# Both products of every join in the third PSUM bank of the MLP, and all steps in a new order

## The chip, the cores and the metric

The kernel runs on one NeuronCore of a Trainium2 chip. The metric is the device time of one execution, in microseconds (us). A kernel is run several times, and its time is the median of the runs. One further execution is profiled by the hardware; its span, clock and single instructions are what the views of the profile show.

The engines are called as in the profile: PE (TensorE matmuls), PEld (its weight loads), DVE (VectorE), ACT (ScalarE), POOL (GpSimd), SP (SyncE, which issues most of the DMAs). A "q" behind the name (SPq, ACTq) is that engine's issuing of DMAs. L856 is line 856 of the kernel.

## The reference, cut to what matters

Four batches, eight heads, 768 tokens, head dimension 48. A DeltaNet recurrence gives x, and an MLP with layer norm and residual works on it:

```python
k_n = k / (norm(k) + 1e-6)
for t in range(768):
    y[t]  = q[t] @ state
    v_old = k_n[t] @ state
    state = state + beta[t] * outer(k_n[t], v[t] - v_old)
x  = y as (4, 768, 384)
xn = (x - mean) / sqrt(var + 1e-6) * g_ln
out = x + maximum(xn @ w_ch1, 0) @ w_ch2      # 384 -> 1536 -> 384
```

All is float32.

## The kernel before

**Chunks.** The tokens are handled in 12 chunks of 64 (all 32 pairs of batch and head at once). Inside a chunk the recurrence is written as a triangular system: the Gram matrix of the keys (`gram`, L786) is stored to HBM and read back in another layout (tile `gb`, eight DMAs on SP, L830), and `rows_inverse` (L822) inverts the two 32x32 diagonal blocks of two chunks at a time, with 31 pairs of VectorE operations one behind the other (the product into `tmp`, L856, and the subtraction from `xb`, L863). The result is stored (`xd`, L867) and read back by DMAs on SP into `xt` (L870). All DMAs go through one helper and so have the line L349.

**The join.** `join(c)` (L879) makes the off-diagonal block of the inverse from the two diagonal ones: a VectorE transpose into `xnj` (L884), 64 matmuls of 32x32 (`prod_e`, L894, called e2 for chunk 2 and so on), four ACT multiplications by -1 into `es` (L906), 64 matmuls again (`prod_z`, L900, called z2), and four ACT copies into `xt` (L912). Both products stand in one PSUM bank, `bank`. Chunks 1 to 5 take `f_[2]`, the third bank of the MLP; from `LATER` = 6 on they take `by[:, 0]`, the first half of the two banks that the recurrence uses for Y.

**The recurrence.** `recur(c)` (L967) has the products keys times state (ks, in `two`) and queries times state (qs, in `by`), both L979, the subtraction from v, the product with the inverse (u, L1013), then the output (y, L1020, in `by`) and the new state (s, L1030, in `two`). The products of queries and keys of a chunk (L771) use `by` too. These, like the join's, are many matmuls on small tiles (64 or 32 wide).

**The MLP.** For chunks 0 to 3 the first layer is a plain product (L1296). From chunk `FROM` = 4 on it is done in fifteen block products on sums of blocks, `fifteen(c)` (L1168): each product is eight matmuls of 128x128 (L1217), and they accumulate in the four banks `f_[2], f_[1], f_[0], f_[3]` (`X`, L1208); products 0, 3, 5 and 8 go to `f_[2]`, and what is in a bank is added up by ACT copies (L1233) and VectorE sums (L1237) into `h_all`. The second layer is done in seven products, `seven(c)` (L1398): each is six steps of two matmuls, 128x192 wide (L1419), in `f_[0]`, `f_[3]`, `f_[1]` for these chunks. Their sums of inputs run on POOL (L1406) or VectorE.

**The order.** Every step is registered with the keys that it reads and writes (`Line.add`, L169); there are 2991. They are issued in the sequence written out in `ORDER` (L59 to 153), in which `z` stands for a filler matmul (`zeros`, L1511). A step can stand anywhere behind those that it depends on, by its keys. `in_this_order` (L26) then pins the queue of each engine to that sequence, with the issues of DMAs in it, so on each engine nothing overtakes. Each MLP step of PE can be put between the steps of the recurrence of the next chunk, and `ORDER` does so nearly everywhere.

**The first inverse.** Chunk 0 has its own inverse, made by doubling on PE (`first_inverse`, L648, products at L720 and L737) in two halves of the heads, g0 and g1. The masks that it needs are made by VectorE (L395, L402) and Pool (L421) in the first ten microseconds. The first `rows_inverse` is that of chunk 1; then come chunks 2 and 3 together, 4 and 5, and so on.

Of the kernel before, what the change touches and what calls it, by code (L numbers as in the profile page):

```python
# [63 lines left out]
146 232 230 149 326 150 219 669 154 z 209 234 155 156 208 231 233 210 158 157 251 46 235 164 160 162 327 200 161 328 239 201 411 159 413 165 170 166  # L64
# [136 lines left out]
def kernel(  # L201
# [26 lines left out]
    FROM, LATER = 4, 6  # L228
# [72 lines left out]
    by = psum.tile([128, 2, 512], FP32, name="by")  # L301
# [20 lines left out]
    ATT = FK[2]  # L322
# [1326 lines left out]
```

## Time and profile before

| what | us |
|---|---|
| median of 3 runs | 508.59 (508.59, 509.01, 507.37) |
| profiled execution | 506.83 |
| its span | 505.1 (1.73 lie around it) |
| PE busy in the span | 485.9 |
| DVE busy | 355.2 |
| POOL busy | 275.7 |
| ACT busy | 249.0 |
| mean granted PE clock | 0.973 |

The chain of work that ended last lies on PE for 78% of the span and on DVE for 13%; 31% of the span is L1419 and 22% is L1217. The DVE part is the inverse (L856 and L863, 4% each), all of it in the first quarter of the span.

A few steps can be followed by their times in the trace. The first tensor operation of the inverse of chunk 1 starts at 35.5 us, its last pass ends at 72.2; that of chunks 2 and 3 starts at 81.3 and ends at 113.7; their reloaded blocks have landed at 123.0, and e2 starts at 123.8. Later joins: e4 at 183.7, e6 at 244.8, e7 at 276.7, e8 at 331.6, e9 at 356.3, e10 at 402.3, e11 at 424.7 us.

In views of groups a row has the line, engine, operation, output and input tiles, the shapes, the count and the durations. In the view of waits a row has the engine and line that waited, what ended the wait, and the total, the number and the longest. In the chain a row has the start, the length and the work.

### The profile page before, as it was taken

What the parts mean: (1) busy time and instruction counts of PE and PEld (TensorE: products, weight loads), DVE (VectorE), ACT (ScalarE), POOL (GpSimd) and SP (SyncE); (2) the same over time, 40 slices, a digit from 0 to 9 for tenths busy, and PEclk for the clock granted to TensorE, in tenths of its full rate; (3) what the DMA queues carried; (4) which work ended last, traced back from release to release, by engine and by line L of the source; (5) the groups of instructions that cost most, each with busy time, mean ns of one, the idle gap of its engine ahead of it and who ended that gap; (6) DMA issues with size and microseconds to landing.
All of it is one profiled execution on the core that took longest, in us unless ns stands there. A gap on an engine that the chain in (4) does not pass through costs nothing.

```text
span 505.1 us, 22184 instructions
## 1 busy us (share of the span) xinstructions
PE 485.9 (96%) x9606; PEld 445.7 (88%) x9606; DVE 355.2 (70%) x774; ACT 249.0 (49%) x620; POOL 275.7 (55%) x430
## 2 busy tenths in 40 slices
PE   6777999999999999999999999999999999999996
PEld 3666988688988898899999999999999999999996
DVE  9689987997699458886559898478899238143251
ACT  5777772633645434636444544436563347363230
POOL 5464527255754595629893462591642851645643
PEclk9776799999999999999999999999999999999999
DMA  8979896756646676448734434765245412111101
GB/s 173 308 153 187 270 189 79 107 138 133 90 87 106 192 127 114 46 100 205 155 41 64 102 55 153 150 91 87 57 85 136 82 23 58 43 50 46 31 12 31
DMA packets 196097, 54.99 MB, mean 109 GB/s; under 512 B 186076, under 2 KB 189404, under 8 KB 196000
## 3 DMA queue, kind: packets, MB, share of 16 engines
q1 hardware_dynamic: 189920, 40.58, 42.1%
q10 hardware_dynamic: 3872, 9.83, 6.1%
q0 software_dynamic: 2208, 3.17, 3.7%
q8 instruction: 75, 1.23, 1.0%
q14 instruction: 22, 0.18, 0.1%
HBM read 36.64 MB, written 16.91 MB: 106 GB/s over the span
## 4 chain that ended last, share of the span: by engine, by line
PE 78%; DVE 13%; SPq 3%; issue 2%; POOL 1%; DMA 1%; ACT 1%; ACTq 0%; DVEq 0%; POOLq 0%
PE f L1419 31%; PE f L1217 22%; PE f L1296 6%; DVE xb L863 4%; DVE tmp L856 4%; SPq L349 3%; PE by L1020 2%; PE two L1013 2%; PE by L979 2%; PE by L771 2%; PE two L979 2%; PE two L1030 1%; PE two L771 1%; PE by L894 1%; PE by L900 1%
## 5 line engine op out<-in xcount | busy, mean ns | idle before, releaser
L1406 POOL TENSOR_TENSOR h_all<-h_all 128x256 f32<-128x256 f32 x123 | 90.2, 746 | 133.3 <-PE f L1419 103.7
L1419 PE MATMUL f<-w_sb,h_all 128*128 128x192 f32 x492 | 109.5, 332 | 0.0
L1419 PE MATMUL f<-words,h_all 128*128 128x192 f32 x396 | 84.5, 330 | 0.3 <-POOL h_all L1406 0.3
L1419 PEld LDWEIGHTS f<-w_sb,h_all 128*128 128x128 f32 x492 | 81.8, 190 | 1.8 <-DVE o L1437 0.2
L863 DVE TENSOR_TENSOR xb<-xb,tmp 128x87 f32<-128x87 f32 (+21 forms) x186 | 73.7, 396 | 4.8
L856 DVE TENSOR_TENSOR tmp<-xb,gb 128x87 f32<-128x87 f32 (+21 forms) x186 | 73.1, 393 | 4.9
L1237 DVE TENSOR_TENSOR h_all<-h_all,f 128x512 f32<-128x512 f32 x96 | 63.6, 682 | 14.2 <-PE f L1217 13.1
L1419 PEld LDWEIGHTS f<-words,h_all 128*128 128x128 f32 x396 | 66.6, 190 | 1.7 <-POOL h_all L1406 1.0
L1296 PE MATMUL f<-xnt,w_sb 128*128 128x256 f32 x216 | 50.2, 382 | 0.0
L349 POOL DMA_DIRECT2D tb<-in_k_dram x64 | 41.9, 660 | 10.3 <-DVE kt L751 9.4
L1239 ACT ACTIVATE h_all<-h_all 128x512 f32<-128x512 f32 x48 | 28.5, 624 | 34.4 <-DVE h_all L1237 34.0
L1296 PEld LDWEIGHTS f<-xnt,w_sb 128*128 128x128 f32 x216 | 40.2, 190 | 5.2
L1233 ACT COPY h_all<-f 128x512 f32<-128x512 f32 x48 | 26.3, 590 | 33.9 <-PE f L1217 17.1
L1437 DVE TENSOR_TENSOR o<-f,x 128x192 f32<-128x192 f32 x33 | 11.6, 352 | 41.8 <-PE f L1419 25.9
L1217 PE MATMUL f<-words,w_sb 128*128 128x128 f32 x256 | 31.7, 276 | 0.0
L1305 ACT ACTIVATE h_all<-f 128x256 f32<-128x256 f32 x36 | 13.4, 383 | 34.8 <-PE f L1296 34.8
L1217 PEld LDWEIGHTS f<-words,w_sb 128*128 128x128 f32 x256 | 30.0, 192 | 0.2
L1217 PE MATMUL f<-xnt,w_sb 128*128 128x128 f32 x192 | 25.4, 276 | 0.0
L542 POOL TENSOR_TENSOR w_sb<-words 128x768 uint32<-128x768 uint32 (+1 forms) x11 | 15.0, 1364 | 17.7 <-DVE words L529 16.7
L1217 PEld LDWEIGHTS f<-xnt,w_sb 128*128 128x128 f32 x192 | 23.7, 192 | 0.1
L1322 PEld LDWEIGHTS f<-xnt,w_sb 128*128 128x128 f32 x144 | 19.5, 203 | 3.4 <-ACT h_all L1330 0.2
L1084 ACT ACTIVATE xnt<-xnt,g_sb 128x256 f32<-128x256 f32 x27 | 12.5, 499 | 19.2 <-DMA xnt<-xld 19.1
(246 smaller groups left out, 955.0 us busy)
## 6 DMA issues: line engine op xcount, KB each, us to landing
words<-in_moe_w_ch_dram ACTq DMA_DIRECT2D x10, 768.0 KB, 7.8
gd<-gsb SPq DMA_DIRECT2D x11, 512.0 KB, 3.9
v<-in_v_dram SPq DMA_DIRECT2D x24, 192.0 KB, 4.2
kr<-in_k_dram SPq DMA_DIRECT2D x46, 96.0 KB, 3.9
out_dram<-o SPq DMA_DIRECT2D x44, 96.0 KB, 2.4
xld<-xlt SPq DMA_DIRECT2D x9, 384.0 KB, 3.0
xnt<-xld SPq DMA_DIRECT2D x36, 96.0 KB, 3.3
gb<-gd SPq DMA_DIRECT2D x44, 64.0 KB, 3.0
```

The costliest lines, as they stand in the source:

```text
L349: add(eng, cost, lambda: QUEUE[eng].dma_start(out=out_, in_=in_), r, w, bulk=n * ns / 16e3, **kw)
L856: lambda j=j, n=n, w=w, t=t: nc.vector.tensor_tensor(out=t, in0=xv[:, 0:n, j : j + 1].to_broadcast([np_, n, w]), in1=gv[:, j : j + 1, j + ...
L863: "DVE", dve(n * w), lambda t=t, rest=rest: nc.vector.tensor_tensor(out=rest, in0=rest, in1=t, op=ALU.subtract),
L979: nc.tensor.matmul(dst[half(e), hp, j], src[drows(hp), (e if n else key_half(c, hp, e)) * GP + j], s_all[drows(hp), e, j], start=(n == 0 o ...
L1217: nc.tensor.matmul(wide(p[:, 128 * n : 128 * n + 128]), w[n // 2][:, n % 2 * 128 : n % 2 * 128 + 128], r, start=start and n == 0, stop=Tru ...
L1233: add("ACT", act(512), lambda: nc.scalar.copy(o, p), pk, ok)
L1237: add("DVE", dve(512), lambda: nc.vector.tensor_tensor(out=o, in0=o, in1=p, op=op), pk, ok)
L1239: add("ACT", act(512), lambda: nc.scalar.activation(o, o, ACTF.Relu), [], ok)
L1296: nc.tensor.matmul(p[:, 0:TOK], w1_sb[:, t, f * 128 : (f + 1) * 128], xnt[:, t], start=(t == 0), stop=(t == KC - 1))
L1322: nc.tensor.matmul(p[:, 0:128], w1_sb[:, t, f * 128 : (f + 1) * 128], xnt[:, t, cols], start=(t == 0), stop=(t == KC - 1))
L1406: add(eng, cost, lambda: e.tensor_tensor(out=out_, in0=x, in1=y, op=op), r, w, port=2 if eng == "Pool" else 1, pr=-2)
L1419: lambda f=f, t=start and f == 0: nc.tensor.matmul(p[:, 0:D2], lhs(f), rhs[:, f], start=t, stop=(f == F2 - 1), skip_group_check=True),
```

## The change

In `join` the choice of the bank by chunk is taken out: `bank` is `f_[2]` for every chunk, and the keys are the outer `ATT = FK[2]` (L322), which name the same bank. The whole of `ORDER` is replaced. The same steps are in it, and a filler `z` stands at two places instead of one. Of each engine's queue most steps have another place: of 817 steps of PE 706, of 774 of DVE 500, of 589 of ACT 503, of 426 of Pool 358, of 386 of SP 363.

```diff
@@ -57,99 +57,99 @@
 ORDER = """
-9 1 50 49 8 63 52 51 10 5 244 54 71 11 56 6 0 14 7 12 62 47 53 48 23 13 72 55 36 18 64 42 26 37 61 27 58 60 77 81 15 28 17 32 325 43 73 88 29 40 65 79
...
-146 232 230 149 326 150 219 669 154 z 209 234 155 156 208 231 233 210 158 157 251 46 235 164 160 162 327 200 161 328 239 201 411 159 413 165 170 166
...
+63 5 50 53 2 3 47 71 52 8 51 6 48 9 10 58 49 11 23 12 13 61 18 38 72 32 54 17 62 33 55 21 30 4 7 27 36 56 19 42 64 14 0 43 60 15 44 20 39 65 77 81 16
...
+107 133 131 216 129 228 229 134 142 208 109 108 144 143 217 198 z 136 218 135 137 249 219 230 247 140 145 147 250 154 671 141 231 248 244 236 155 413
+148 210 327 232 199 149 420 237 146 238 59 150 158 328 233 151 326 46 160 223 239 200 152 340 153 162 202 156 234 159 41 170 157 161 251 235 221 201
+212 381 268 339 349 z 214 331 414 269 385 379 189 419 416 194 270 226 350 196 197 353 271 272 382 333 273 355 274 357 275 195 383 276 358 277 390 351
...
@@ -877,7 +877,7 @@
     def join(c, **kw):
-        bank, ATT = (f_[2], FK[2]) if c < LATER else (by[:, 0], BY[:2])
+        bank = f_[2]
         gs, xt = gsbs[c % NG], xts[c % NX]
```

By the keys of the steps, the products e and z of chunks 6 to 11 stood before in sequence with the recurrence's and the queries' products in `by`; after the change they stand in sequence with products 0, 3, 5 and 8 of `fifteen` in `f_[2]`. For chunk c that means behind the last drain of product 8 of chunk c-2 and, with the copies into `xt`, ahead of product 0 of chunk c-1. In the order of before, product 0 of chunks 7 and 9 stands ahead of e8 and e10; in the new one it stands behind z8 and z10.

180 rows, old and new, of the table ORDER are left out of this document.

## The prediction

> **What bounds the kernel now.** I read the page first, then the windows (busy time of each engine by stretch), the waits of TensorE and the chain that ended last. The page:
>
> ```profile
> PE 485.9 (96%) x9606; PEld 445.7 (88%) x9606; DVE 355.2 (70%) x774; ACT 249.0 (49%) x620; POOL 275.7 (55%) x430
> ```
>
> TensorE (PE) is nearly always busy, so what counts is where it is not. The windows give start:end, length, then busy time (instructions) of PE, PEld, DVE, ACT and POOL, the granted PE clock, the DMA share and GB/s:
>
> ```profile
> 0.00:50.00 50.00, 36.05 (x972) 28.42 (x976) 40.98 (x110) 34.02 (x82) 26.37 (x43) 0.78 0.92 207
> 50.00:55.00 5.00, 4.97 (x92) 4.39 (x85) 4.97 (x9) 4.00 (x11) 3.18 (x3) 0.50 0.75 206
> 60.00:120.00 60.00, 60.00 (x1144) 48.60 (x1144) 52.82 (x125) 29.86 (x86) 29.45 (x41) 1.00 0.70 132
> 120.00:140.00 20.00, 19.48 (x457) 17.34 (x455) 12.31 (x27) 10.77 (x31) 14.76 (x22) 1.00 0.64 91
> 160.00:320.00 160.00, 160.00 (x3382) 150.38 (x3372) 120.53 (x259) 79.41 (x197) 94.94 (x151) 1.00 0.56 114
> 320.00:480.00 160.00, 160.00 (x2872) 154.88 (x2865) 91.59 (x184) 74.98 (x178) 84.40 (x139) 1.00 0.34 69
> ```
>
> From 160 to 480 us PE is busy 320.00 of 320 us at full clock. There only the sum of PE's own work sets the end. Some 14 us are idle in the first 50, and half a microsecond at 120 to 140. The waits of TensorE (waiting line, what ended it: total, times, longest) say what the late one is:
>
> ```profile
> PE f L771 <- issue: 2.4, 1, 2.4
> PE f L894 <- DVE xnj L884: 0.4, 1, 0.4
> ```
>
> Every wait longer than 0.5 us stands before 60 us. The 0.4 is the join of chunk 2 (e2), and the chain (start, length, what) shows on what it hangs:
>
> ```profile
> 113.53 0.22 DVE xb L863
> 113.80 0.34 SPq L349
> ...
> 120.03 2.98 DMA xt<-xd
> 123.03 0.72 DVE xnj L884
> 123.80 0.75 PE f L894 x50
> 124.55 2.15 PE f L1419 x12
> 126.70 0.68 PE f L900 x50
> 127.38 2.47 PE f L1419 x14
> 129.85 1.08 PE two L1013 x64
> 130.93 1.50 PE f L1419 x8
> ```
>
> So there are two regimes. Up to e2 at 123.8 us, VectorE's inverse (L856/L863), its store and its loads give the pace, and PE would have come only 0.4 us earlier. After e2 all is PE, one step behind the other. The end is the time of e2 plus the PE work after it plus whatever stalls the new order adds.
>
> **The change part by part.** No step is added or removed but one filler, so the sum has four terms.
>
> *The bank.* For chunks 6 to 11 the join no longer holds Y's bank. The waits of TensorE name that bank (by) only for lines of the start (L568, L720, L737), and PE is at 160.00 of 160. Worth nothing: 0.
>
> *The price of the sequence.* PE steps have fixed start-to-start times in the dense part. In the chain above 14 matmuls of L1419 (seven steps of two) take 2.47 us and 8 (four steps) take 1.50: a step is 0.97/3 = 0.325, and a block of them between small-tile steps (joins and recurrence, 32- or 64-wide) carries 2.47 - 7 x 0.325 = 0.20 more. Two 64-wide steps in a row save 0.145 together (at 175.7 us the chain has one at 1.08 and the next at 0.93). Counted in both orders: up to e2 there are 16 entries into small tiles before and 14 after, and 2 neighbouring pairs against 4: -2 x 0.20 - 2 x 0.145 = -0.69 us. After e2 there are 55 entries against 52, and 19 pairs against 17: -3 x 0.20 + 2 x 0.145 = -0.31 us. The first amount lies before e2, where VectorE's chain gives the pace: counted at 0 (bounds -0.4 and 0, since PE is only 0.4 early there). The second counts whole: **-0.3**.
>
> *The start.* The time of e2 follows the first VectorE inverse (its first tensor op at 35.5 us), and from there to the last pass before e2 the VectorE queue holds 74.34 us of work and waits before, and by the same rows 74.07 in the new order (-0.27): no shift by itself. What moves is the stretch before 35.5. For the worse: of the key loads of chunk 0 one is issued behind one of chunk 1 (an SP issue is 0.6 to 0.8 us), and the setting up on Pool (0.62 us a copy), that VectorE's mask operations wait for, is drawn out by about 1.4 us; this bounds it at +1.5. For the better: in the doubling steps of the first inverse (L720/L737, 0.7 to 1.1 us each at this clock) the first half of the heads now goes ahead of the second instead of taking turns, which I add up to 2.7 us by its third step; less what comes late, this bounds it at -2.5. The 2.41 us "issue" stall at 22.17 us, an instruction fetch in the middle of this chain, may move or stay. In the middle: **-0.5**. The additional filler (1.22 us at half clock for the one at 30.3 us) falls where PE waits anyway: 0, and 1.2 if the start leaves no such gap.
>
> The clock is at 0.50 from 42.0 to 55.7 us, though PE is busy 4.97 of 5 us from 50 to 55. The Trainium skill ("TensorE: Matmul & The Clock Gate", What's actually happening) says that full clock comes after one busy window of about 3.4 us, and that the windows run freely. The six changes of clock in the trace are whole multiples of 3.41 us apart, which agrees. By that rule a denser start could get full clock one window earlier, and PE would gain half of 3.41 = 1.7 us; by the row of e2 it gains nothing while VectorE is the later one, so the sum stays as it is.
>
> *The waits that the shared bank makes.* The third MLP bank (f_[2]) carries products 0, 3, 5 and 8 of each chunk from 4 on. So e(c) and z(c) must now lie between the draining of product 8 of chunk c-2 and product 0 of chunk c-1, and that product waits for the four XT copies. Their prices:
>
> ```profile
> L906 ACT ACTIVATE es<-by x24: 373/375/377, 245.7 to 427.4; 32x256 f32<-32x256 f32 x24
> L912 ACT COPY xt<-by x24: 362/363/366, 252.0 to 431.2; 32x256 f32<-32x256 f32 x24
> ```
>
> Four copies are 4 x 0.363 = 1.45 us, four multiplications 1.50. I added up the PE steps that the new order puts between. From z to product 0: 13.8 us for chunk 6, 6.9, 3.0, 14.5, 2.7 and 11.4 for 11: all above 1.45, the least with 1.2 to spare. From e to z: 4.4, 10.1, 2.7, 4.2, 1.8 and 4.5, against 1.50; only chunk 10 is tight (0.3 to spare, 2.15 us of cover before). If ACT is in the middle of something else (a 128x512 copy is 0.59), 0.3 at each tight place. Behind product 0 stand all PE steps, as its queue is in order; nothing runs around it.
>
> The other way in which the order pays: e(c) must come sooner. The PE work ahead of e4 falls by 5.1 us, of e8 by 3.1, e9 3.6, e10 2.7, while VectorE's work ahead of the inverse for chunks 4 and 5 falls by 0.2 only. Before, the reloaded block for e4 landed at 178.8 us, its transpose takes 0.7, and e4 ran at 183.7: 4.2 us to spare. 5.1 - 4.2 is a stall of up to 0.9; one load fewer stands ahead of it on SP (0.6). For e8 3.0 us were to spare against 3.1. I take 0.4 at e4, 0.4 at the joins of 8 and 10 together: **+0.8**, bounds 0 and +2.7 (0.9 and six times 0.3).
>
> The sum: 506.83 (profiled execution: span 505.1 and 1.73 around it) - 0.5 - 0.3 + 0.8 = 506.8, no change. The profiled run lies 1.76 under the median, so on the median's scale this is 508.6. A measurement here tells about 0.3% (1.5 us) from nothing: faster is below 507.1, slower above 510.1.
>
> **The rivals.**
>
> *Faster: the start comes early and nothing takes it back.* First inverse -2.5, price -0.3 and the -0.4 before e2, stalls 0: 505.4. For it: the idle 14 us all lie there, and the new order moves whole steps in it. Against it: PE's own arrival at e2 is just 0.4 us ahead, so the start must be early for PE too.
>
> *Slower: the start comes late.* Place: VectorE's masks and the first key transposes before 15 us, held by Pool's copies and SP's order. If the first doubling step is 1.4 us late and the better grouping gives nothing back, +1.5 - 0.3 + 0.8 = +2.0: 510.6; with a second instruction fetch as long as the one shown (2.4), 513.0. It decides as soon as VectorE's first inverse starts over 1.0 us later than 35.5. Against it: what I add up of the first inverse favours the new order.
>
> *Slower: the bank.* Place: e and product 0 of chunks 6 to 11 and e4. If ACT and VectorE do not move forward with the joins, all of the +2.7 is paid, with the start at -0.5: +1.9, 510.5. It decides when a copy or a transpose ends over 1.2 us (z10) or 0.3 us (e10) later than its four in a row. For it: the old order had joins 8 and 10 behind product 0, and the new one can't. The Trainium skill ("PSUM — Partial Sum Buffer", PSUM bank collisions raise a hardware error) says that two engines may not use a bank on the same 32 partitions at once, and that accesses are to be guarded by bank; by it the copies can't overlap product 0 even in other columns, and the wait is whole. No trace here shows such an overlap. Against it: the covers above.
>
> *The change of bank does nothing:* by the first term this is so, and it is part of my forecast.
>
> **How the numbers follow.** No change (507.1 to 510.1 by itself): 0.30. Faster by the start: 0.26. Slower by the start 0.24, by the bank 0.20. A little of the forecast and of the bank's case lies over the bounds: faster 0.27, same 0.29, slower 0.44. The ends: all favourable bounds together -3.2, with 0.4 for the spread of the runs, 505.0; the late start with the stalls at their upper bound, +1.5 - 0.3 + 2.7 = +3.9, or with a fetch, 513.0.
>
> **What would show it.** In the changed profile PE must again be 160.00 of 160 in the late windows, e2 should fall at 123.3 +- 2, and the work from e2 to the end be 0.3 us shorter. The start is read from the first tensor op of the inverse (35.5 before). The bank is read from waits of L894, L900 and L1217 on ACT's L906 and L912 and on L884: under 0.5 each. I am wrong if a wait of more than 1 us stands after e2, if the first inverse moves by over 2.5 us, or if the clock rises a window earlier and e2 follows it.

## The result, and the profile after

The changed kernel takes 515.12 us (median of 5 runs, 514.03 to 515.96) against 508.59 before; the ratio of the two is 1.0122, with a 95% interval of 1.0095 to 1.0149. It is slower by some 6.2 us, outside my range (505.0 to 513.0), and on the side to which I had given 0.44. The profiled execution took 515.05 us with a span of 513.2, so it is 8.2 us above the profiled one of before, which lay 1.8 us under its own median.

The page, and the windows in the same columns as before:

```profile
PE 484.9 (94%) x9608; PEld 443.1 (86%) x9608; DVE 355.9 (69%) x774; ACT 247.6 (48%) x620; POOL 278.2 (54%) x430
```

```profile
0.00:50.00 50.00, 32.16 (x881) 23.57 (x881) 38.27 (x103) 34.31 (x79) 25.69 (x41) 0.91 0.89 201
50.00:55.00 5.00, 5.00 (x158) 4.35 (x158) 4.49 (x12) 2.43 (x8) 1.12 (x3) 0.54 1.04 214
55.00:60.00 5.00, 3.52 (x71) 2.66 (x67) 4.33 (x11) 3.88 (x8) 1.37 (x1) 0.80 1.01 291
120.00:140.00 20.00, 18.12 (x391) 16.56 (x392) 12.30 (x24) 6.06 (x17) 13.51 (x20) 1.00 0.75 122
160.00:320.00 160.00, 157.37 (x3378) 147.15 (x3376) 121.34 (x255) 75.99 (x195) 102.66 (x162) 1.00 0.57 112
320.00:480.00 160.00, 160.00 (x2887) 154.24 (x2880) 94.47 (x193) 75.47 (x179) 80.86 (x131) 1.00 0.35 74
```

PE works no longer (484.9 us against 485.9). It is idle in more places: in the first 50 us, at 55 to 60, at 120 to 140, and for 2.6 us between 160 and 320, where there had been nothing. The waits of TensorE name them:

```profile
PE by L568 <- DVE xb L402: 4.8, 1, 4.8
...
PE by L1020 <- issue: 1.1, 1, 1.1
PE two L1013 <- ACT xt L912: 1.1, 1, 1.1
PE by L979 <- DVE pt L802: 1.0, 1, 1.0
...
PE f L1217 <- POOL ident L1193: 0.8, 1, 0.8
PE f L1296 <- DVE o L1437: 0.8, 1, 0.8
```

(A letter and a number name a product and its chunk: u2 is the product with the inverse for chunk 2, y5 and s5 are the output and the new state of chunk 5, E1 and E3 the first and third doubling steps of the first inverse.) The first wait is at 4.9 to 9.7 us, in the first key transpose. The one of L979 is at 120 us, just ahead of e2. The other four (u2 at 134, the step after e5 at 202, y5 at 230, the step after e6 at 251 us) lie behind e2. None is product 0 waiting for a join's copies (L1217 on L912), the wait that the shared bank was to bring.

Following single steps through both traces divides the 8 us. E1, the first doubling step, starts at 16.9 us (13.5 before), the first inverse at 38.8 (35.5), e2 at 128.9 (123.8): **5.1 us are lost before e2**. From e2 to the last PE step are 379.65 us (376.55): **3.1 us are lost behind it**. The price of the steps there, by their own start-to-start times, is 374.58 against 374.88; what is left, PE's stalls, is 5.1 us against 1.7. This divides one profile of each kernel; the runs below show how far the two numbers can be trusted.

The chain shows the loss at the start (start, length, work):

```profile
4.11 5.17 DVE xb L402 x3
9.28 0.06 issue
9.34 0.27 DVE kr L360
...
9.72 1.09 PE by L568 x4
...
22.65 5.78 DMA gd<-gsb
...
29.91 6.60 DMA gb<-gd
```

Three L402 operations on 128x64 integers, 0.2 us each when nothing disturbs them, last until 9.28 us (one of them alone from 4.26), just when Pool's last instruction of the setting up ends (9.23). Behind them on VectorE stand the memsets that pad the key tiles of chunk 0 (L360), and the first transpose on PE needs these. Before, the memsets were among VectorE's first instructions (0.9 and 1.7 us) and the transpose started at 5.96. The Gram matrix of chunk 1 is stored at 22.65 (16.21 before), and the inverse needs it back.

### The profile page after: what moved, and what is told of

The parts are those of the page before. It is cut to its first block, busy times and chain, and to the rows that moved or that the text cites. A ratio compares the mean times of both kernels' runs of the same rounds, so it can differ in the third digit from the quotient of the medians.

```text
span 513.2 us, 22166 instructions
## 1 busy us (share of the span) xinstructions
PE 484.9 (94%) x9608; PEld 443.1 (86%) x9608; DVE 355.9 (69%) x774; ACT 247.6 (48%) x620; POOL 278.2 (54%) x430
## 4 chain that ended last, share of the span: by engine, by line
PE 73%; DVE 8%; DMA 6%; SPq 5%; ACT 3%; issue 2%; POOL 2%; ACTq 0%; POOLq 0%; DVEq 0%
PE f L1419 27%; PE f L1217 20%; SPq L349 5%; PE f L1296 4%; PE f L1322 3%; PE f L1337 3%; DVE tmp L856 3%; DVE xb L863 3%; PE by L1020 2%; DMA gb<-gd 2%; PE two L1013 2%; PE two L979 2%; PE by L979 2%; PE by L771 2%; PE two L1030 1%
## 5 line engine op out<-in xcount | busy, mean ns | idle before, releaser
L1419 PE MATMUL f<-words,h_all 128*128 128x192 f32 x396 | 87.0, 331 | 0.0
L863 DVE TENSOR_TENSOR xb<-xb,tmp 128x87 f32<-128x87 f32 (+21 forms) x186 | 76.5, 411 | 4.6
L856 DVE TENSOR_TENSOR tmp<-xb,gb 128x87 f32<-128x87 f32 (+21 forms) x186 | 74.2, 399 | 5.0
L1296 PEld LDWEIGHTS f<-xnt,w_sb 128*128 128x128 f32 x216 | 40.1, 190 | 6.2 <-DVE o L1437 0.9
L1437 DVE TENSOR_TENSOR o<-f,x 128x192 f32<-128x192 f32 x33 | 11.7, 354 | 48.2 <-PE f L1419 31.8
L1233 ACT COPY h_all<-f 128x512 f32<-128x512 f32 x48 | 26.4, 588 | 25.2 <-PE f L1217 13.5
L906 ACT ACTIVATE es<-f 32x256 f32<-32x256 f32 x44 | 16.5, 375 | 34.0 <-PE f L894 33.5
L1217 PE MATMUL f<-words,w_sb 128*128 128x128 f32 x256 | 32.3, 276 | 0.0
L1217 PEld LDWEIGHTS f<-words,w_sb 128*128 128x128 f32 x256 | 30.3, 192 | 0.2
L1058 ACT ACTIVATE x<-by 128x384 f32<-128x384 f32 x23 | 11.1, 490 | 31.7 <-PE by L1020 17.5
L1217 PE MATMUL f<-xnt,w_sb 128*128 128x128 f32 x192 | 25.4, 276 | 0.0
L1217 PEld LDWEIGHTS f<-xnt,w_sb 128*128 128x128 f32 x192 | 23.7, 192 | 0.1
L1322 PEld LDWEIGHTS f<-xnt,w_sb 128*128 128x128 f32 x144 | 18.1, 191 | 3.5 <-ACT h_all L1330 0.3
```

The costliest lines, as they stand in the source:

```text
L856: lambda j=j, n=n, w=w, t=t: nc.vector.tensor_tensor(out=t, in0=xv[:, 0:n, j : j + 1].to_broadcast([np_, n, w]), in1=gv[:, j : j + 1, j + ...
L863: "DVE", dve(n * w), lambda t=t, rest=rest: nc.vector.tensor_tensor(out=rest, in0=rest, in1=t, op=ALU.subtract),
L1217: nc.tensor.matmul(wide(p[:, 128 * n : 128 * n + 128]), w[n // 2][:, n % 2 * 128 : n % 2 * 128 + 128], r, start=start and n == 0, stop=Tru ...
L1233: add("ACT", act(512), lambda: nc.scalar.copy(o, p), pk, ok)
L1296: nc.tensor.matmul(p[:, 0:TOK], w1_sb[:, t, f * 128 : (f + 1) * 128], xnt[:, t], start=(t == 0), stop=(t == KC - 1))
L1322: nc.tensor.matmul(p[:, 0:128], w1_sb[:, t, f * 128 : (f + 1) * 128], xnt[:, t, cols], start=(t == 0), stop=(t == KC - 1))
```

## The experiments

Each edit keeps the steps and moves some in `ORDER` by their numbers, or changes the bank. In the names of MLP steps F4.12 is product 12 of `fifteen(4)`, V3.4c the third step of product 4 of `seven(3)`, and M3.2 a step of the plain first layer of chunk 3. Comparisons are with runs of before on the same chip (medians 509.0, 508.9 and 508.4 us in the three series). "e2" is its start in the one profile of the kernel; "rest" is from there to the last PE step.

| kernel | median us | ratio to before | 95% | e2 | rest |
|---|---|---|---|---|---|
| before | 508.59 | 1 | | 123.8 | 376.6 |
| the change | 515.12 | 1.0122 | 1.0095 to 1.0149 | 128.9 | 379.7 |
| bank_only | 515.95 | 1.0130 | 1.0094 to 1.0167 | 123.6 | 384.4 |
| bank_four | 509.94 | 1.0018 | 0.9997 to 1.0040 | 124.3 | 378.1 |
| head_before | 511.04 | 1.0039 | 1.0018 to 1.0059 | 125.3 | 380.1 |
| head_after | 514.77 | 1.0100 | 1.0062 to 1.0138 | 126.8 | 379.1 |
| pads_first | 512.66 | 1.0079 | 1.0050 to 1.0107 | 127.3 | 378.9 |
| pool_late | 513.43 | 1.0106 | 1.0077 to 1.0135 | 128.6 | 378.7 |
| gram_early | 519.24 | 1.0208 | 1.0171 to 1.0244 | 133.6 | 379.2 |
| gram_again | 511.86 | 1.0051 | 1.0020 to 1.0083 | 123.7 | 378.8 |
| rest_fixed | 509.44 | 1.0018 | 0.9997 to 1.0040 | 124.7 | 378.5 |
| split_y5 | 509.03 | 1.0011 | 0.9984 to 1.0038 | 126.0 | 377.8 |
| all_fixed | 517.02 | 1.0175 | 1.0137 to 1.0213 | 132.1 | 377.8 |
| all_again | 510.41 | 1.0027 | 0.9994 to 1.0059 | 126.5 | 377.3 |

### The bank without the new order

bank_only takes the order of before and moves only what has to stand later:

```diff
-        bank, ATT = (f_[2], FK[2]) if c < LATER else (by[:, 0], BY[:2])
+        bank = f_[2]
 ORDER of before; products 0 and 3 of fifteen(7) and fifteen(9) and their
 ACT copies now behind the copies of z8 and z10, product 0 of fifteen(5)
 behind those of z6
```

> The order of before with the third MLP bank for all joins; eight steps (products 0 and 3 of fifteen for chunks 7 and 9 with their copies, product 0 of chunk 5) stand later, behind the copies of the join. If the time went to the order and not to the bank: within 0.5 us of before, 508.6, and e2 at 123.8. If the shared bank makes PE wait (the rival of the prediction): 510.5, with waits of L1217 or L894 on L906 or L912 after 240 us.

It came out at 1.0130, as slow as the whole change and some 5 us over what I had expected if the bank cost time, with e2 where it was. The waits of TensorE in its profile:

```profile
PE f L1217 <- ACT xt L912: 2.1, 2, 1.2
...
PE f L1217 <- ACT h_all L1233: 1.6, 2, 0.8
```

So the bank does cost, in an order that was not made for it. Product 0 waits for the join's copies (1.40 us at chunk 7, 0.98 at chunk 5, by start-to-start times, which hold a little more than the idle time in the rows), and then product 3 for the copy that drains product 0, as the two now stand side by side (1.02 and 1.01). PE's stalls behind e2 are 9.5 us against 1.7. My edit put the moved steps at the first place open to them; a better place may hide part of it. bank_four leaves out the two joins that product 0 used to overtake:

```diff
+        bank, ATT = (f_[2], FK[2]) if c not in (8, 10) else (by[:, 0], BY[:2])
 ORDER of before, product 0 of fifteen(5) behind z6's copies
```

> The order of before with f_[2] for the joins of chunks 6, 7, 9 and 11 and Y's bank for 8 and 10, and one step (product 0 of chunk 5) behind z6's copies. If what the bank cost in bank_only (7.6 us in the profile) belongs to joins 8 and 10, which product 0 used to overtake: one wait of 1.0 us at product 0 of chunk 5, and 509.5 to 510. If every join pays for the shared bank: 512 or more.

One wait of 0.99 us at product 0 of chunk 5, and the rest 378.1: 1.5 us more than before, against 7.8 more in bank_only. Six of the 7.8 us belong to joins 8 and 10. The ratio (1.0018) is not clear of 1.

### Before e2 or behind it

The two orders have nearly the same steps ahead of e2 (13 differ, none of them on PE, and the second filler), so they can be joined there.

```diff
 head_before: ORDER of before up to e2, then the change's order of what is left; bank f_[2]
 head_after:  ORDER of the change up to e2, then before's order of what is left; Y's bank
```

> Every step up to e2 in the order of before, all later ones in the order of the change, bank f_[2]. If 5 of the 8 us of the profile were lost before e2: e2 at 123.8, and the time 510 to 511. If the later order with the shared bank carries the loss: 513 or more.

> Every step up to e2 in the order of the change, all later ones in the order of before, with Y's bank for chunks 6 to 11. If the loss is before e2: e2 at about 128.9 and the time 512.5 to 514. If it is in the later order: 509 to 510.

head_before loses 0.4%, 2.0 us; head_after 1.0%, 5.1 us. The parts add up to more than the whole (7.1 against 6.2) because the seam of head_after has a stall of its own (1.85 us at 141 us). Taking head_before's 2.0 from 6.2, some 4 us are lost ahead of e2, where no step uses another bank than before. The profiles don't fix this share: e2 was at 123.6 to 126.0 us in the six kernels with the order of before up to it, and at 128.9 and 126.8 in the two with the change's (the change and head_after). The means are 3.2 us apart, so 5.1 is the upper end of what the start may have lost.

### The start

pads_first moves two steps of VectorE in the changed kernel:

```diff
 ORDER, VectorE's steps
-5 2 3 47 10 11 23 12 13 18 17 21 30 4 27 19 14 0 15 20 16 75 89 1 76
+5 1 0 2 3 47 10 11 23 12 13 18 17 21 30 4 27 19 14 15 20 16 75 89 76
```

> The changed kernel with two VectorE steps, the memsets of the key tiles' padding of chunk 0 (L360), moved to the front of VectorE's queue, as in before. If these memsets, queued behind the slow L402 operations, made the start late: the first L568 transpose at 6.6 instead of 9.72 us, e2 3 to 4 us earlier than 128.85, and the time 511 to 512. If the start is late by the loads or by the whole of Pool and VectorE (masks): under 1 us gained, 514 or more.

The first transpose as the timeline has it (start, length, work, idle time and what ended it):

```profile
6.71 0.63 PE L568 MATMUL by<-ident,kr 128*128 128x128 f32 x4 [1.94 <-DMA kr<-in_k_dram]
```

The transposes start 3.0 us earlier, now behind their load; E1 is at 14.3 (16.9). By e2 1.5 us of it are left, and the ratio falls from 1.0122 to 1.0079, 2.2 us; the intervals of the two just overlap. So the memsets are most likely a part, and the first reading (3 to 4 us at e2) was too much: the Gram store is still at 20.0 us (16.2 before), and the first inverse at 38.45. pool_late asks why L402 takes so long. It moves one Pool step:

```diff
 ORDER, Pool's steps
-40 245 ... 246
+40 ... 246 245
```

> The changed kernel with one Pool step, the memset of a q/k tile (L1536, 0.94 us), behind the memset of the inverse (from 8.29 to about 20 us). If VectorE's three L402 operations (5.17 us at 4.1) last as long as Pool is working beside them: they end 0.9 us earlier, at 8.35, and the first transpose starts at 8.8 instead of 9.72. If they are slow by themselves: no change, 9.28.

VectorE's timeline now has

```profile
4.02 4.36 DVE L402 TENSOR_SCALAR xb<-xb 128x64 int32<-128x64 int32 x2
```

which ends at 8.38, 0.9 us earlier, when Pool's last copy ends (8.33). L402 was held until Pool stopped. This agrees with the Trainium skill ("SBUF — State Buffer", Who interferes with whom): a VectorE tensor_scalar in a two-port mode and a Pool instruction can't hold the port pair at once. That L402 runs in such a mode is not shown here. The Trainium skill has the lock held for one instruction; here VectorE got no turn between Pool's queued ones. In the kernel of before one L402 was let go in the middle of Pool's setting up, at 6.18 us, when Pool had turned from its copies to issuing a DMA (5.86 to 6.48). The transpose came at 9.30 instead of 9.72, as the memset of its pad (8.93) still stands behind other VectorE steps. In the total, 1.0106 against 1.0122, this cannot be told from nothing.

gram_early puts the Gram matrix of chunk 1 forward:

```diff
 ORDER of pads_first
+filler 73 ahead of the first transpose; ACT's key copy 79 ahead of mask copies 34, 35
+ACT's Gram copies 103, 104 and their store 105 ahead of back copies and conversions
+weight loads 66, 68, 69 behind the store
```

> pads_first with the Gram matrix of chunk 1 put forward: the filler ahead of the first transpose, ACT's first key copy ahead of the mask copies, ACT's two Gram copies (L792) and the store to HBM ahead of weight conversions and back copies, three weight loads behind that store. If what is left of the late start is this chain (store, reload, inverse): the store at 16 to 17 us instead of 20.0, the first inverse at 35 to 36, and 1.5 to 2.5 us less than pads_first. If the reload takes as long as other loads make it (7 + 6 us), or fetches decide: under 1 us less.

The store came at 18.2 us, but the time rose to 519.24:

```profile
PE by L737 <- ACT xt L679: 10.1, 1, 10.1
```

My edit had made this wait: ACT's weight conversions kept their places, the loads that they need were now late, and the back copies of the first inverse (L679) stood behind them on ACT. It says nothing on either reading. gram_again leaves the weight loads alone:

```diff
 ORDER of pads_first
+filler 73, ACT's 79, 103, 104 and the store 105 as in gram_early; weight loads not moved
```

> pads_first with the filler ahead of the first transpose, ACT's first key copy ahead of the mask copies, and ACT's two Gram copies and the store ahead of back copies and conversions; the weight loads stay where they are in pads_first (gram_early moved them, and ACT's conversions then waited for them, with the back copies behind). If the store, reload and inverse carry the rest of the late start: the store at 17 to 18 us (20.0 in pads_first), first inverse at 36 to 37, 1 to 2 us less than pads_first. If the start is set by PE's and ACT's doubling steps: under 0.5 less.

The store is at 18.9, the first inverse at 36.1 and e2 at 123.7, as in before; the ratio is 1.0051, 1.4 us under pads_first, which is inside the two intervals. But this profile was the fastest of the kernel's ten runs (509.02, with a median of 511.86), and all_again below, whose steps up to e2 stand in the same order, had e2 at 126.5. How much of the late start this edit brings back is therefore not shown. The rest (378.8) is still the change's.

### Behind e2

Three stalls recur at the same steps in every kernel with the change's order there. For the step after e5 (M3.2), the timelines of VectorE and Pool show what delayed the sum L1437 that frees its bank:

```profile
199.22 1.46 DVE L856 TENSOR_TENSOR tmp<-xb,gb 128x135 f32<-128x135 f32 x1
200.71 1.57 DVE L863 TENSOR_TENSOR xb<-xb,tmp 128x135 f32<-128x135 f32 x1
202.32 0.32 DVE L856 TENSOR_TENSOR tmp<-xb,gb 128x156 f32<-128x156 f32 x1
...
202.91 0.35 DVE L1437 TENSOR_TENSOR o<-f,o 128x192 f32<-128x192 f32 x1
```

```profile
198.69 1.93 POOL L349 DMA_DIRECT2D tb<-in_k_dram  x3
200.63 1.49 POOL L622 TENSOR_TENSOR v<-v,knrm 128x768 f32<-128x768 f32 x1
```

What the sum reads was there at 198.7 us, when a sum on Pool ended, but from 199.2 on four inverse operations stood before it, and two of them took 1.5 us instead of 0.3. The second (200.71) ran beside L622 on Pool. The first (199.22) ran beside three DMA issues on Pool, and these don't explain it: in before the same operation took 0.30 us (at 195.22) beside such issues. Why it was slow stays open; the edit below only moves the sum ahead of it. For the step after e6 (F4.12) it is Pool's own queue:

```profile
250.40 0.68 POOL L349 DMA_DIRECT2D tb<-in_k_dram  x1
251.10 0.74 POOL L1163 TENSOR_TENSOR q_last<-q_last,w_sb 128x256 f32<-128x256 f32 x1
251.79 0.46 POOL L1193 TENSOR_TENSOR ident<-xnt,words 128x128 f32<-128x128 f32 x1
```

The sum of weights (L1163) that F4.12 multiplies with was made at 182.9 us in before; in the new order it is made 0.5 us ahead of its use. At y5 nothing was late:

```profile
229.33 1.10 PE L1020 MATMUL by<-u,pt 64*64 64x48 f32 x60
231.53 0.32 PE L1020 MATMUL by<-u,pt 64*64 64x48 f32 x4 [1.09 <-issue]
```

PE stops four matmuls from the end; a 16 KB packet on the "instruction" queue starts at 229.1, under s5.

```diff
 rest_fixed: ORDER of head_before
+VectorE's sum 1090 (L1437) ahead of four inverse operations
+Pool's 1271 (L1163) and 1442 (L1193) ahead of the DMA issue 2040
+loads 1846, 1860, 1861 (v and q of chunk 7) behind the inverse's store 1195
```

> head_before (the order of before up to e2, of the change behind it) with three local moves: VectorE's sum L1437 of chunk 2 ahead of four inverse operations, Pool's operations 1271 (L1163) and 1442 (L1193) ahead of a DMA issue, and three loads of v and q for chunk 7 behind the store of the inverse (some 10 us later). If the three PE stalls after e5, y5 and e6 (0.83, 1.33, 0.67 us in head_before) come from these places: all three gone, 2 to 2.9 us less than head_before, no slower than before. If the stall at y5 is a fetch of instructions that does not depend on the loads: only 1.5 less, and 1.3 still there. If the shared bank is what costs: under 0.5 less.

The stalls after e5 and e6 are gone; the one at y5 is 1.06 us (0.8 of idle time in the waits), though its fetch (at 224.3 us) has hardly another transfer beside it any more. The rest is 1.6 us shorter, and the ratio 1.0018. So the loads were not the cause at y5. split_y5 takes the two small-tile steps apart:

```diff
 ORDER of rest_fixed, PE's steps
-s5 y5 V3.4c V3.2f V3.4d V3.5d V3.4e V3.5e V3.4f F4.0
+s5 V3.4c V3.2f V3.4d V3.5d V3.4e V3.5e V3.4f F4.0 y5
 and the two ACT steps that read y5 (1397, 1399) behind it
```

> rest_fixed with the output product y5 eight PE steps later, so that it does not follow s5 at once (both are 64 matmuls on small tiles). If the stall at y5 (1.06 us in rest_fixed, ended by nothing but an instruction fetch of 16 KB that begins under s5) comes from two steps of many short instructions behind the start of a fetch: it is gone, and the stretch from e2 to the end is 1.0 us shorter, 377.4. If the fetch stalls PE wherever it falls: the same 1 us at another step.

The wait is gone (y5 now runs its 64 matmuls in one piece), though the fetch still begins under s5, at 225.5 us; the wait did not appear elsewhere in that stretch. The rest is 377.8, 0.7 shorter and not 1.0, since the pair's saving (0.145) and one more change between wide and small tiles (0.20) are paid. The ratio is 1.0011; so small a gain can't be told in the medians.

That two small-tile steps behind the start of a fetch always stop PE is not so. In pads_first a fetch of 16 KB begins at 152.58 us, two such steps follow at once, and nothing stops:

```profile
152.70 1.15 PE L979 MATMUL by<-s_all,qt 48*64 48x48 f32 x64
153.68 1.25 PE L1013 MATMUL two<-v,xt 64*64 64x48 f32 x64
154.85 3.50 PE L1296 MATMUL f<-xnt,w_sb 128*128 128x256 f32 x15
```

What sets y5 apart from this pair is open.

### All together

Both take the change's own order and add the edits up.

```diff
 all_fixed: ORDER of gram_early, with the moves of rest_fixed
 all_again: ORDER of gram_again, with the moves of rest_fixed and split_y5
```

> The order of the change with all of these moves: pads first, Gram early, and the three local ones. If the loss is made up of these places, one behind the other: 508 to 509.5, as before. If the shared bank carries part of it: 511 or more.

> The order of the change with all moves: pads, Gram (gram_again), three local ones, y5 split. If the loss is the sum of these places: 508 to 509.5. If a part of it lies with the shared bank: 511 or more.

all_fixed repeats the fault of gram_early (e2 at 132.1), while its rest is 377.8. all_again is at 1.0027 (0.9994 to 1.0059): 4.8 us of the 6.2 are recovered, with f_[2] in all joins and 16 steps moved in the change's order, and its interval lies wholly under that of the change. So most of the loss was in the places of these steps, with the shared bank left as it was. The wait at u2 is still there (0.5 us). No version came out clearly under before, so none beats both kernels.

## Why the prediction was wrong

**The start was the term that failed:** I had put it at -0.5, with an upper bound of +1.5; at e2 it was +5.1 in the profile, and +3 to +4 by the other readings (the means of e2, and the 6.2 of the medians less head_before's 2.0). The bound held SP's one issue and Pool's longer set-up (1.4 us, and VectorE was indeed held, until 9.28 instead of 7.2). What I did not do was to read VectorE's own queue in the new order: two memsets behind the held operations, and PE's first transpose behind these. That made E1 3.4 us late. I had also followed only the doubling steps, where the new grouping does help (the first half's E3 is at 28.7, 29.3 before), and not the chain beside them: ACT's second Gram copy 2.2 us behind the first, the store 6.4 us late, the first inverse 3.3. That VectorE's queue keeps its length up to e2 (-0.27) was wrong too: its last pass there is 4.6 us late, having been 3.3 late at the beginning.

**The price of the sequence was right:** from e2 on it is 374.58 us against 374.88, the -0.3 of the sum.

**The waits of the shared bank were right where I looked, but the term of the stalls failed too, at other steps.** The covers between z and product 0 held, also for chunk 10, and e4 did not wait. But I allowed +0.8 only at those places. The 3.4 us of new stalls came from steps whose slack the order had used up: a sum on VectorE, a weight sum on Pool, a fetch under two small-tile steps, and at u2 the join's copies (L912, from 134.49 us), which stand on ACT behind the square root (L835, at 134.21) of the next inverse, whose reload came late. No run takes the wait at u2 apart. The largest number that I allowed for the stalls (+2.7) was a count of joins; it should have been a count of all steps with under a microsecond between their maker and PE.

**Y's bank:** that freeing it is worth nothing agrees with all runs, as no kernel is clearly faster. That "the change of bank does nothing" holds only with a new order; bank_only pays 6 to 7 us for it. There product 0 waited for the join's copies to end, but the keys of the steps demand this; no run shows what the bank itself would do.

**The rivals:** the late start came, as named, but with 5.1 us where its term was 1.5; its condition, a first inverse over 1.0 us late, was met by 3.3. Two of the three signs of being wrong came: the first inverse moved by over 2.5 us, and two waits of over 1 us stand behind e2 (u2 and y5). The upper end of 513.0 took the late start with a second fetch, but not the stalls at their bound as well. The rival of the bank came only in bank_only. The clock was higher in the first 50 us (0.91 instead of 0.78) and lower from 55 to 60 (0.80 instead of 0.93); e2 came late all the same.

**Left open:** whether the later order had to be worse because of the bank, or only came out so. The three stalls behind e2 that were undone had nothing to do with f_[2], but the joins that stand earlier (e4 by 5.1 us of PE work) took the room of other steps; no run separates that. Of the late start, the part of the memsets is just not clear of the noise, and the part that is ACT's (gram_again against pads_first) shows in one profile, not in that of all_again, and is not clear in the medians.

## What to carry to other kernels

When a whole order changes, go through the queue of every engine for the first steps that PE needs, and list for all of PE's steps the slack to their maker: two memsets of 0.27 us each behind a held operation cost about 2 us here (pads_first). A bank shared between two users costs what its drains leave uncovered, and this was 7 us in one order and nothing that the waits show in another. Where PE stops and the profile names nothing that it waited for, look for an instruction fetch, and try to take the steps around it apart: at y5 this removed the stop.

## What the runs showed of the hardware

- A VectorE operation that takes 0.2 us alone was held for 5.0 us (4.1 in pool_late) while Pool worked through a row of queued instructions, and was let go within 0.1 us of Pool's end (9.28 after 9.23, 8.38 after 8.33). In before one was let go earlier, at 6.18 us, while Pool issued a DMA.
- In eight kernels an instruction fetch of 16 KB began near s5, with y5 right behind, and PE stopped four matmuls before the end of y5 (0.8 to 1.1 us of idle time), with other transfers beside the fetch or nearly none; with eight wide steps between s5 and y5 it did not stop. It is no rule for every such pair: the two steps at 152.70 us in pads_first ran through.
- Kernels with the same order up to e2 (bank_only, bank_four, head_before, rest_fixed, split_y5) had e2 at 123.6 to 126.0 us. That is about as much as the runs of one kernel differ (507.4 to 509.6 for before), so most of that spread can come from the start. Other pairs with one order up to e2 differ as much: 128.9 and 126.8 (the change and head_after), 123.7 and 126.5 (gram_again and all_again). The stretch behind e2 is closer: 378.7 to 380.1 us in the six kernels with the change's order there and nothing moved in it (the change, head_before, pads_first, pool_late, gram_early, gram_again).
